# Key weights in four loads, and a new table of engine orders, in a linear-attention and gMLP kernel

## The chip, the core and the metric

The kernel runs on one core of one Trainium2 chip. Its engines are TensorE (PE, matmuls, with the loading of its weights, PEld, as a stream of its own), VectorE (DVE), ScalarE (ACT), GpSimd (POOL) and SyncE (SP, which here only issues transfers). The metric is the device time of one execution in microseconds (us). It was 242.62 us before the change, the median of three runs (242.23, 242.62 and 243.85).

## What is computed

Two residual blocks follow each other on x of 2048 rows by 512 columns. H is 32 heads of 16 columns, F is 1792 and Fh is 896.

```python
h  = x + A(layernorm(x))
h2 = h + B(layernorm(h))

def A(x):                         # linear attention
    q, k, v = split(x @ wqkv)     # 32 heads of 16 columns each
    phi = lambda t: where(t > 0, t + 1, exp(t)) + 1e-6
    kv  = einsum('bhsd,bhse->bhde', phi(k), v)
    z   = sum of phi(k) over the rows
    return ((phi(q) @ kv) / (phi(q) @ z + 1e-6)) @ wo

def B(x):                         # gMLP with a spatial mix
    z  = gelu(x @ w_in)           # 1792 columns
    z1, z2 = z[:, :896], layernorm(z[:, 896:])
    g  = w_sp @ z2 + b_sp         # w_sp is 2048 x 2048
    return (z1 * g) @ w_out
```

## The kernel before, in words

The 2048 rows are 16 tiles of 128 rows, and four groups of four tiles. Everything stays in SBUF between the load of x and the store of the result. The stages, as TensorE sees them:

- Start. Ten matmuls on a constant keep TensorE busy (L563). x arrives in loads of one, two or four tiles (the function `load_x`, issued at L495). DVE takes the statistics of each tile (L575 for the sums, L579 to put them together), the reciprocal standard deviation comes from ACT for the first four tiles (L589, L591) and from POOL for the others, in pairs (L594 adds epsilon, L596 raises to a power), and DVE normalises (L610). Tiles 0 to 3 are transposed by TensorE (L644, copied out by ACT at L651), the other twelve by transfers that SP issues (L636).
- Projections. K is x times the key weights, tile by tile (L732), and Q is computed transposed, by groups of rows (L746). ACT takes the exponential and the positive part (L709, L711) and DVE puts phi together (L712 clamps, L715 adds, L718 does the sum with a selection for pairs without a positive part from ACT). phi(k) times x is accumulated over all tiles (L764).
- The small matrices. The sum z (L776, L789), the products with the value weights (L813) and with wo (L832), the denominators (L852, their logarithm and exponential on ACT at L857 and L860), and a spreading of the reciprocals over the heads (L868, copied out by ACT at L872), by which DVE scales phi(q) (L876).
- The attention's output (L898), to which DVE adds x (L903). For the second layernorm DVE takes statistics (L575, L579), POOL makes the scale and the shift of two tiles with four instructions (L594, L596, L625, L626), ACT applies them (L617), and SP transposes the result into hT by a transfer (L636).
- z2 (L930, gelu by ACT at L935, layernorm by DVE at L939, L579 and L610 with POOL's L594 and L596), and z1 transposed (L961, gelu by ACT at L966).
- The spatial mix (L1000, its sum and product by DVE at L1007 and L1009) and the output projection (L1018, the residual at L1024, the store at L1026).

The matrix w_sp comes in by 64 transposing transfers of one 128 by 512 block each (L976), all issued by SP, 16 for each of four groups of output rows; the mix of a group waits for its 16. POOL issues the large plain loads: the value weights, wo and w_in when the last transfer that transposes x has landed, and w_out and the bias b_sp when the last transfer into hT has landed.

No planner runs when the kernel is built. The program is recorded as some 790 operations with their dependences, and a list written out in the file, ORDER, gives the order in which they are put on their engines' queues. A second list, SLOT, gives the buffer that each temporary tile takes (PSUM banks, the buffers of phi, and so on), in the order of their first use. Each engine runs its queue strictly in that order, and waits on semaphores where the data or a buffer is not there yet. The schedule does not look at costs: the numbers beside the operations (`act_c`, `dve_c`, `MM`) fill in times that decide nothing on the chip.

The loads at the start are these. SP issues x0, x2, x3, the query weights and the rest of x, and ACT issues x1 and the key weights, which are one load of 512 KB:

```python
    load_x("sp", 0, 1)
    load_x("act", 1, 2)
    load("act", "wk", wqkv[:, D:2 * D], w3[:, :, D:2 * D], D * D * 2)
    load_x("sp", 2, 3)
    load_x("sp", 3, 4)
    load("sp", "wq", wqkv[:, 0:D], w3[:, :, 0:D], D * D * 2)
```

## Time and profile before

| | |
|---|---|
| median of three runs | 242.62 us (242.23 to 243.85) |
| the profiled execution's own time | 243.94 us |
| its span, first to last instruction | 242.2 us, at a mean granted TensorE clock of 1.000 |
| VectorE busy, from 10 to 25 us | 5.00, 4.67 and 5.00 of each 5.00 us |
| matmuls of the spatial mix (L1000, two groups of rows) | 73.5 and 24.3 us busy |
| transfers that transpose into hT | 16, in the median 2.5 us from issue to landing |

The profiled execution took 243.94 us, 1.32 us more than the median of the runs without a profile and 1.74 us more than its own span. In a row of a timeline the first number is the start in us from the start of the span and the second the time to the end of the last instruction of that row; then come engine, source line, operation, what is written and read, the shapes, and the number of instructions. Brackets tell how long the engine was idle before and what ended that. A `q` behind an engine's name marks its issuing of transfers, which is not counted as busy. Matmuls overlap, so of four of 512 columns that start at 65.01 the next group can start at 65.87. A row of DMA issues ends with the median time in us from issue to landing.

Of the kernel before, what the change touches and what calls it, by code (L numbers as in the profile page):

```python
# [10 lines left out]
P = 128  # L11
# [1 line left out]


ORDER = [
# [34 lines left out]
]  # L50
SLOT = [
# [6 lines left out]
]  # L58


# [95 lines left out]
class Program:  # L156
# [14 lines left out]
    def op(self, eng, cost, fn, r=(), w=(), bias=0.0, after=(), dma=None, nbytes=0, land=2.0, lag=None,  # L171
           mode=0):
        o = Op()
        o.eng, o.fn, o.cost, o.seq = eng, fn, cost, len(self.ops)
        o.bias, o.land, lag = bias + self.bias, land, self.LAG[eng] if lag is None else lag
        o.late, o.start, o.mode = self.late, None, mode
        o.after, o.deps, o.tiles = list(after) + self.first_of.get(eng, []), {}, []
        o.marked, o.sem, o.semval, o.grp, o.bytes, o.lag = False, None, None, dma, nbytes, lag
        o.raw = set()
        for x in list(r) + list(w):  # L180
            t = getattr(x, "tile", None)
            if t is not None and t not in o.tiles:
                o.tiles.append(t)
                t.ops.append(o)
        rk = [k for x in r for k in x.keys]
        wk = [k for x in w for k in x.keys]
        for k in rk:
            p = self.writer.get(k)
            if p is not None:
                o.deps[p] = True  # L190
                o.raw.add(p)
        for k in wk:
            p = self.writer.get(k)
            if p is not None:
                o.deps[p] = True
            for q in self.readers.get(k, ()):
                if q is not o:
                    o.deps[q] = True
        for k in rk:
            self.readers.setdefault(k, []).append(o)  # L200
        for k in wk:
            self.writer[k] = o
            self.readers[k] = []
        self.ops.append(o)
        return o
# [149 lines left out]
def bass_sequential_preLN__linear_attn_block__mixer_gmlp__prompt_kernel(  # L355
# [11 lines left out]
    _, S, D = A_x.shape  # L367
# [4 lines left out]
    NT, KD, KF, NG = S // P, D // P, FH // P, S // GW  # L372
# [36 lines left out]
    wqkv = View(s_w3, 0, [KD, 3 * D], BF16)  # L409
# [84 lines left out]
    def load(eng, name, dst, src, nbytes, bias=0.0, behind=(), cost=0.5):  # L494
        o = op(eng, cost, lambda e: e.dma_start(dst.ap(), src), w=[dst], dma=(name, False), nbytes=nbytes,  # L495
               bias=bias, land=2.3)
        for p in behind:
            o.deps[p] = True
        return o

    w3 = A_wqkv.rearrange("(c p) f -> p c f", p=P)
# [3 lines left out]
    def load_x(eng, a, b, bias=BIG, **kw):  # L505
        more = {2: 40e3, 3: 60e3, 4: 70e3}.get(a, 0)
        xl[a] = load(eng, f"x{a}", x[a:b, :], x_dram[a * P:b * P, :].rearrange("(n p) d -> p n d", p=P),
                     int((b - a) * P * D * 2 + more), bias, **kw)

    load_x("sp", 0, 1)  # L510
    load_x("act", 1, 2)
    load("act", "wk", wqkv[:, D:2 * D], w3[:, :, D:2 * D], D * D * 2)
    load_x("sp", 2, 3)
    load_x("sp", 3, 4)
    load("sp", "wq", wqkv[:, 0:D], w3[:, :, 0:D], D * D * 2)
    for a in (4, 6):
# [141 lines left out]
    for grp in LN1:  # L658
# [3 lines left out]
        for n in grp:  # L662
# [6 lines left out]
            if n in CENTRED:  # L669
                m, c = st_x[n, 6:7], xc[n, :]  # L670
# [426 lines left out]
```

### The profile page before, as it was taken

Reading aid. Unit: us, or ns where it says so; the run is one execution under the profiler, and the core shown is the slowest. Engines: PE = TensorE matmul, PEld = TensorE weight load, DVE = VectorE, ACT = ScalarE, POOL = GpSimd, SP = SyncE. Lnnn points to the kernel's source line nnn. Section 1 sums busy time; section 2 is a strip of 40 time slices with the busy share of each in tenths; the row PEclk is TensorE's granted clock in tenths of the full one; section 3 lists DMA queues with packets and bytes.
Section 4 is the critical chain, followed back from the end, with each engine's and each line's share of the span. In section 5 each row is a group of like instructions: output and inputs, shape, how many; then the busy total and the mean of one; then the engine's idle time right before and its main releaser. Section 6 shows DMA issues by size and latency. Waiting matters only on the chain.

```text
span 242.2 us, 3056 instructions
## 1 busy us (share of the span) xinstructions
PE 236.3 (98%) x1191; PEld 109.8 (45%) x1191; DVE 132.7 (55%) x269; ACT 78.9 (33%) x101; POOL 36.8 (15%) x84
## 2 busy tenths in 40 slices
PE   7999999999699999999999999999999999999996
PEld 2444444544344445544444444444444444444443
DVE  4899864599967972779505333252332523322443
ACT  3794663777646798464240000000000000000000
POOL 5131314004341420436100000000000000000000
PEclk9999999999999999999999999999999999999999
DMA  6933249991543324597443444442000200000022
GB/s 219 300 79 55 43 89 244 318 132 27 64 88 69 82 46 87 103 301 112 95 108 89 91 106 104 92 110 86 0 0 0 65 24 0 0 3 0 0 87 87
DMA packets 56702, 21.83 MB, mean 90 GB/s; under 512 B 50704, under 2 KB 55824, under 8 KB 56688
## 3 DMA queue, kind: packets, MB, share of 16 engines
q1 hardware_dynamic: 54928, 16.62, 31.8%
q0 software_dynamic: 944, 4.33, 5.7%
q10 hardware_dynamic: 816, 0.70, 0.9%
q8 instruction: 9, 0.15, 0.3%
q14 instruction: 5, 0.04, 0.1%
HBM read 7.47 MB, written 2.10 MB: 40 GB/s over the span
## 4 chain that ended last, share of the span: by engine, by line
PE 91%; DMA 3%; DVE 2%; POOL 1%; ACT 1%; issue 0%; ACTq 0%
PE ps L1000 40%; PE ps L1018 10%; PE ps L961 10%; PE ps L930 9%; PE ps L764 6%; PE ps L732 6%; PE ps L746 5%; PE ps L898 4%; DMA hT<-xn 2%; DVE small L575 1%; DMA xh<-in_A_x_dram 1%; ACT xn L617 1%; DVE xh L903 1%; PE ps L832 0%; PE ps L776 0%; PE ps L813 0%
## 5 line engine op out<-in xcount | busy, mean ns | idle before, releaser
L1000 PE MATMUL ps<-wsp,pk_xn_z 128*128 128x512 bf16 x336 | 73.5, 379 | 0.0
L1007 DVE TENSOR_TENSOR e<-ps,e 128x512 bf16<-128x512 f32 x28 | 19.3, 691 | 67.4 <-PE ps L1000 67.4
L1000 PEld LDWEIGHTS ps<-wsp,pk_xn_z 128*128 128x128 bf16 x336 | 32.9, 98 | 39.7
L930 PE MATMUL ps<-win,hT 128*128 128x512 bf16 (+1 forms) x128 | 26.0, 353 | 1.9 <-DMA hT<-xn 1.9
L961 PE MATMUL ps<-hT,win 128*128 128x512 bf16 x112 | 26.1, 379 | 0.0
L1018 PE MATMUL ps<-wout,xT_pq_z 128*128 128x512 bf16 (+2 forms) x119 | 24.7, 366 | 0.0
L1000 PE MATMUL ps<-wqkv_wsp,pk_xn_z 128*128 128x512 bf16 x112 | 24.3, 379 | 0.0
L939 DVE BATCH_NORM_STATS2 small<-pk_xn_z 128x6 f32<-128x512 bf16 (+1 forms) x32 | 18.2, 607 | 9.0 <-ACT pk_xn_z L935 9.0
L575 DVE BATCH_NORM_STATS2 small<-xh 128x6 f32<-128x512 bf16 x32 | 21.0, 676 | 3.8 <-DMA xh<-in_A_x_dram 3.7
L709 ACT ACTIVATE e<-ps 128x1024 bf16<-128x1024 f32 x16 | 16.4, 1025 | 12.1 <-PE ps L732 7.6
L930 PEld LDWEIGHTS ps<-win,hT 128*128 128x128 bf16 x128 | 12.4, 98 | 14.4 <-ACT xn L617 2.0
L966 ACT ACTIVATE xT_pq_z<-ps 128x1024 bf16<-128x1024 f32 (+1 forms) x16 | 14.2, 917 | 11.4 <-PE ps L961 11.4
L1018 PEld LDWEIGHTS ps<-wout,xT_pq_z 128*128 128x128 bf16 x119 | 11.5, 98 | 13.0
L1024 DVE TENSOR_TENSOR e<-ps,xh 128x512 bf16<-128x512 f32 (+2 forms) x17 | 11.2, 660 | 11.3 <-PE ps L1018 11.3
L596 POOL TENSOR_TENSOR small<-small 128x2 f32<-128x2 f32 x22 | 17.0, 792 | 1.1
L1000 PEld LDWEIGHTS ps<-wqkv_wsp,pk_xn_z 128*128 128x128 bf16 x112 | 11.0, 98 | 13.2
L935 ACT ACTIVATE pk_xn_z<-ps 128x896 bf16<-128x896 f32 x16 | 14.3, 918 | 8.1 <-PE ps L930 8.0
L961 PEld LDWEIGHTS ps<-hT,win 128*128 128x128 bf16 x112 | 11.0, 98 | 12.7
L594 POOL TENSOR_SCALAR small<-small 128x2 f32<-128x2 f32 x22 | 6.7, 307 | 65.9 <-DVE small L579 65.8
L764 PE MATMUL ps<-pk_xn_z 128*128 128x512 bf16 x64 | 16.2, 379 | 0.0
L732 PE MATMUL ps<-wqkv_wsp,xT_pq_z 128*128 128x512 bf16 x64 | 15.9, 379 | 0.0
L746 PE MATMUL ps<-xT_pq_z,wqkv_wsp 128*128 128x512 bf16 x64 | 15.5, 380 | 0.0
(71 smaller groups left out, 181.8 us busy)
## 6 DMA issues: line engine op xcount, KB each, us to landing
out_dram<-e SPq DMA_DIRECT2D x15, 128.0 KB, 1.7
win<-in_B_w_in_dram POOLq DMA_DIRECT2D x1, 1792.0 KB, 12.3
xh<-in_A_x_dram SPq DMA_DIRECT2D x4, 256.0 KB, 6.7
wout<-in_B_w_out_dram POOLq DMA_DIRECT2D x1, 896.0 KB, 6.3
wsp<-in_B_w_sp_dram SPq DMA_TRANSPOSE x48, 2.7
wqkv_wsp<-in_A_wqkv_dram ACTq DMA_DIRECT2D x1, 512.0 KB, 4.5
wqkv_wsp<-in_A_wqkv_dram SPq DMA_DIRECT2D x1, 512.0 KB, 6.1
xh<-in_A_x_dram SPq DMA_DIRECT2D x1, 512.0 KB, 7.4
```

The source lines that it names most:

```text
L575: op("dve", dve_c(512), lambda e: e.bn_stats(s6.ap(), src.ap()), r=[src], w=[s6])
L596: return op("pool", 0.665, lambda e: e.tensor_tensor(dst.ap(), dst.ap(), h.ap(), ALU.pow), r=[dst, h], w=[dst])
L709: op("act", act_c(n), lambda e: e.activation(lo.ap(), t(flat).ap(), ACT.Exp), r=[t()], w=[lo])
L732: i = e.matmul(t(bank(ti)).ap(), lhsT=lhs.ap()[:, c, :], rhs=rhs.ap()[:, c, :], start=(c == 0), stop=(c == KD - 1))
L746: r_ = e.matmul(t(bank(i)).ap(), lhsT=lhs.ap()[:, c, :], rhs=rhs.ap()[:, c, :], start=(c == 0), stop=(c == KD - 1))
L764: r = e.matmul(txk[h](bank(i)).ap(), lhsT=xx.ap()[:, c * P:(c + 1) * P], rhs=kk.ap(), start=(n == 0), stop=(n == NT - 1))
L930: k = e.matmul(t(bank(i)).ap()[:, 0:b - a], lhsT=l.ap()[:, c, :], rhs=win[c, a:b].ap(), start=(c == 0), stop=(c == KD - 1))
L939: op("dve", dve_c(b - a), lambda e, s6=s6, src=src: e.bn_stats(s6.ap(), src.ap()), r=[src], w=[s6])
L961: k = e.matmul(t(bank(i)).ap(), lhsT=l.ap()[:, c, :], rhs=r_.ap()[:, c, :], start=(c == 0), stop=(c == KD - 1))
L1000: k = e.matmul(t(bank(0)).ap(), lhsT=l.ap()[:, s - a, :], rhs=r_.ap()[:, s - a, :], start=(s == 0), stop=(s == NT - 1))
L1007: op("dve", dve_c(512), lambda e: e.tensor_tensor(gb().ap(), t(bank(0)).ap(), bsp().ap()[:, tg * GW:(tg + 1) * GW], ALU.add), r=[t(), bsp( ...
L1018: k = e.matmul(t(bank(0)).ap()[:, 0:b - a], lhsT=l.ap()[:, fc, :], rhs=wout[fc, a:b].ap(), start=(fc == 0), stop=(fc == KF - 1))
```

## The change

The key weights come in four loads of 128 KB, one for each 128 rows of the weight matrix, all issued by ACT, and x1 moves from ACT to SP:

```diff
     load_x("sp", 0, 1)
-    load_x("act", 1, 2)
-    load("act", "wk", wqkv[:, D:2 * D], w3[:, :, D:2 * D], D * D * 2)
+    load_x("sp", 1, 2)
     load_x("sp", 2, 3)
+    for c in range(KD):
+        load("act", f"wk{c}", wqkv[c, D:2 * D], w3[:, c, D:2 * D], P * D * 2)
     load_x("sp", 3, 4)
     load("sp", "wq", wqkv[:, 0:D], w3[:, :, 0:D], D * D * 2)
 ORDER = [
-    0, 3, 4, 11, 13, 14, 1, 2, 5, 6, 7, 8, 9, 10, 16, 12, 37, 38, 27, 28, 29, 30, 31, 32, 33, 34, 21, 44, 26, 39, 40,
+    0, 1, 30, 31, 32, 33, 3, 34, 4, 5, 6, 35, 40, 41, 16, 17, 21, 2, 7, 8, 9, 29, 42, 43, 10, 11, 12, 13, 24, 14, 15,
...
```

The whole of ORDER and SLOT is replaced. No operation is added or taken away beside the three loads, so what changes is the place of each operation on its engine's queue, and the buffers. The places that matter below:

- TensorE. All four K products of tiles 0 to 3 now come before the first Q product. Between the product with wo (L832) and the first attention output (L898) stands one Q product instead of two, and between the second pair of denominators (L852) and its spreading (L868) one attention output instead of two. Behind the z2 product of tile 0 (L930, eight matmuls) came the z2 product of tile 1; now two attention outputs (L898, eight matmuls) stand between them. In both orders 352 matmuls stand ahead of tile 0's z2 product.
- DVE. The last normalisations of x come ahead of the phi of K's tiles 8 and 9, and between the statistics of attention tiles 0 and 1 stands a clamp (L712).
- POOL. The order of the large loads was value weights, wo, w_in; it is now w_in, value weights, wo. The building of the matrix for the spreading (L548, L550) moves from the start to between and behind these loads. The load of the bias b_sp comes nine operations of L594 and L596 later behind that of w_out.
- SP. Ahead of the first transfer into hT stand 13 transfers of w_sp instead of 11. The other three of the first sixteen now stand together between the fifteenth and the sixteenth transfer into hT, where they were five, spread over three places.
- ACT. The gelus and normalisations of the second half are in another order.

Lines of the changed kernel behind the loads are one higher than those given here.

72 rows, old and new, of tables (ORDER, SLOT) are left out of this document.

## The prediction

> **What bounds the kernel now.** I read the page's table of engines and its row of the granted clock first, then the waits of TensorE, then TensorE's timeline from 58 to 72 us, where its only waits of any size lie, then the chain of waits of that stretch and its transfers, and last the start and POOL's queue.
>
> ```profile
> PE 236.3 (98%) x1191; PEld 109.8 (45%) x1191; DVE 132.7 (55%) x269; ACT 78.9 (33%) x101; POOL 36.8 (15%) x84
> PEclk9999999999999999999999999999999999999999
> 58.38 0.62 PE L852 MATMUL ps<-xT_pq_z,small 128*32 128x256 bf16 x16
> 58.93 1.90 PE L898 MATMUL ps<-pk_xn_z,xT_pq_z 128*128 128x512 bf16 x8
> 60.82 0.61 PE L868 MATMUL ps<-wsp 128*128 128x128 bf16 x8
> 61.65 1.69 PE L930 MATMUL ps<-win,hT 128*128 128x512 bf16 x8 [0.23 <-DMA hT<-xn]
> 65.01 1.02 PE L930 MATMUL ps<-win,hT 128*128 128x512 bf16 x4 [1.68 <-DMA hT<-xn]
> 65.87 1.03 PE L898 MATMUL ps<-pk_xn_z,xT_pq_z 128*128 128x512 bf16 x4
> 66.74 0.81 PE L930 MATMUL ps<-win,hT 128*128 128x384 bf16 x4
> ```
>
> TensorE is 98% busy at full clock, and the change neither adds nor removes a matmul. So only TensorE's idle time can be won. After its first K product at 6.87 it waits twice to speak of: 0.23 us ahead of z2 of tile 0 and 1.68 ahead of z2 of tile 1. Tile 0's eight matmuls cost 0.86 (65.01 to 65.87, four of 512 columns) and, for its four of 384 columns, three quarters of 0.87 (65.87 to 66.74), 0.65, so 1.51 together. They could have been over at 61.65 + 1.51 = 63.16, and tile 1 starts at 65.01: 1.85 us lost. With the 0.23, some 2.1 us, 0.9% of the time, is all that the change can win.
>
> ```profile
> 52.44 1.24 DVE xh L903
> ...
> 55.30 0.86 POOL small L594
> ...
> 57.70 0.63 POOL small L626
> 58.35 1.52 ACT xn L617 x2
> ...
> 60.45 4.43 DMA hT<-xn
> ```
> ```profile
> hT<-xn SPq DMA_TRANSPOSE x1, 2.4
> ```
> ```profile
> q8 instruction: 1, 0.02, 2.9%
> ```
>
> This chain of waits releases tile 1. Its last step is a transfer that took 4.43 us. The one before it, for tile 0, issued in 59.00 to 60.42 and shown second, took 2.4. The third fence is the table of DMA queues from 62 to 64: one packet of 20 KB of instructions or less was fetched just then, behind which part of the late transfer stood. At 2.4 us tile 1 would have landed at 62.85 and nothing would have been lost. So 1.85 us hangs on one accident of a profiled execution, which took 243.94 us, 1.32 above the median. I do not know whether it is in the unprofiled runs (242.23, 242.62, 243.85 differ by as much), and count two thirds of it there: 1.24 us in the median.
>
> **The change, part by part.** *Start.*
>
> ```profile
> 3.38 0.69 DVE L575 BATCH_NORM_STATS2 small<-xh 128x6 f32<-128x512 bf16 x1 [3.38 <-DMA xh<-in_A_x_dram]
> 4.39 0.29 ACT L589 ACTIVATE small<-small 128x1 f32<-128x1 f32 x1 [1.39 <-DVE small L579]
> 4.21 0.66 DVE L575 BATCH_NORM_STATS2 small<-xh 128x6 f32<-128x512 bf16 x1
> 5.38 0.66 DVE L575 BATCH_NORM_STATS2 small<-xh 128x6 f32<-128x512 bf16 x1
> 6.48 0.66 DVE L575 BATCH_NORM_STATS2 small<-xh 128x6 f32<-128x512 bf16 x1
> 6.87 1.03 PE L732 MATMUL ps<-wqkv_wsp,xT_pq_z 128*128 128x512 bf16 x4
> 1.23 0.46 ACTq L495 DMA_DIRECT2D wqkv_wsp<-in_A_wqkv_dram  x1
> 1.72 1.28 ACT L554 ACT_TABLE_LOAD   x1 [1.72 <-PEq L1082]
> ```
> ```profile
> xh<-in_A_x_dram SPq DMA_DIRECT2D x2, 128.0 KB, 3.5
> wqkv_wsp<-in_A_wqkv_dram ACTq DMA_DIRECT2D x1, 512.0 KB, 4.5
> ```
>
> The first K product follows x0's statistics at 3.38 through normalising, transposing and copying, and x0 is still the first load. ACT now issues four loads, the first in place of x1, so the second ends at 1.69, the last 2 x 0.46 later at 2.61, and the table load at 3.9, ahead of 4.39. The key weights landed at 1.23 + 4.5 = 5.73; with x1 and x2 six pieces of 128 KB came in behind x0's 3.38, 0.39 us each. Now x0, key piece, x1, key piece and so on alternate. At 0.39 each x1 lands at 4.2, x2 at 4.9, x3 at 5.7 and the last key piece at 6.1, against uses at 4.21, 5.38, 6.48 and 6.87. I cost the start at 0; the cover is these margins, and where it is gone, one issue (0.46) goes straight onto the path: 0 to +0.45. SP's queue issues x1 as well, so query weights and later x leave up to 0.45 later. The query weights have gained time, as all four K products now stand ahead of the first Q: 0.
>
> *POOL's loads* are one queue, with a new order.
>
> ```profile
> 36.29 0.98 POOL L495 DMA_DIRECT2D wqkv_wsp<-in_A_wqkv_dram  x1 [4.87 <-DMA xT_pq_z<-pk_xn_z]
> 37.28 0.76 POOL L495 DMA_DIRECT2D wqkv_wsp<-in_A_wo_dram  x1
> 38.03 0.75 POOL L495 DMA_DIRECT2D win<-in_B_w_in_dram  x1
> ```
> ```profile
> win<-in_B_w_in_dram POOLq DMA_DIRECT2D x1, 1792.0 KB, 12.3
> wqkv_wsp<-in_A_wqkv_dram POOLq DMA_DIRECT2D x1, 512.0 KB, 5.0
> wqkv_wsp<-in_A_wo_dram POOLq DMA_DIRECT2D x1, 512.0 KB, 6.2
> ```
> ```profile
> 45.47 1.06 PE L813 MATMUL ps<-wsp,wqkv_wsp 128*128 128x128 bf16 x16
> 47.77 1.06 PE L832 MATMUL ps<-wqkv_wsp,wsp 128*32 128x512 bf16 x16
> ```
> ```profile
> 27.21 0.43 DVE L712 TENSOR_SCALAR e<-e 128x1024 bf16<-128x1024 bf16 x1 [0.54 <-ACT e L709]
> 27.67 1.23 DVE L718 SCALAR_TENSOR_TENSOR pk_xn_z<-ps,e 128x1024 bf16<-128x1024 f32 x1
> ```
>
> The three landed 4.95, 7.2 and 14.04 us behind the first issue (38.03 + 12.3 = 50.33). In proportion to bytes win alone takes 1792/2816 x 14.04 = 8.9 and each small one 2.5. The small ones now come last: from 36.29, value weights near 47.8 and wo at 50.33. Their products stood at 45.47 and 47.77. By matmuls ahead they move to about 46.3 and 48.4, so TensorE would lose up to 1.9 us (all of it by wo). But the last normalisations of x no longer stand behind a clamp and a sum (0.43 + 1.23 = 1.66), so the last transposes, and the loads, can start up to 1.7 earlier. Then 0.2 is left. The cost lies between 0 and 1.9; I take 0.4, nearer to the early start, since the queue order that makes it is certain and only POOL's part of that chain can spoil it. Building the spreading matrix behind these loads, and b_sp nine operations later, fall in time that POOL idles (15% busy): 0.
>
> *The chain to z2 of tile 0.*
>
> ```profile
> 55.70 0.42 DVE L712 TENSOR_SCALAR e<-e 128x1024 bf16<-128x1024 bf16 x1
> ```
> ```profile
> 77.33 0.22 POOL L594 TENSOR_SCALAR small<-small 128x2 f32<-128x2 f32 x1 [6.88 <-DVE small L579]
> ...
> 78.73 0.20 POOL L626 TENSOR_TENSOR small<-small 128x2 f32<-128x2 f32 x1
> ```
> ```profile
> 34.82 19.90 SPq L976 DMA_TRANSPOSE wsp<-in_B_w_sp_dram  x11
> ```
>
> One clamp (0.42) now stands among the statistics of the pair, and the step at 55.30 begins near 55.75. Matmuls ahead of z2 of tile 0 stay 352, so its wait grows by this: +0.45 (0 if the chain beats TensorE by other means, 0.9 if two such operations slip in). POOL's four instructions took 3.03 us there (55.30 to 58.33) and 1.6 at 77.33 to 78.93, alone. I keep 3.03, since DVE again adds and clamps beside them. The Trainium skill, "SBUF — State Buffer", section Who interferes with whom, says that a DVE instruction with two SBUF inputs, or in a two-port mode, shares ports with POOL's reads. By that rule POOL stays slow and the sum stands; by the calm row tile 0 would land 1.4 earlier and 0.45 would go. SP has 13 w_sp transfers ahead of tile 0's instead of 11, at 1.81 each (19.90/11): begun at 34.8 they are out by 58.4, before ACT's first half at 58.35 + 0.76 = 59.1, and cost 0.
>
> Behind z2 of tile 0 now stand eight attention matmuls: 2 x 0.87 = 1.73 us of cover. Even a transfer of 4.4 us hardly shows: -1.85 in the profile, -1.24 in the median.
>
> *The rest.* One attention product instead of two between denominators and spreading, and gelus in another order: margins of tenths, no priced wait. From nothing to a few; I take one wait like the smallest seen, +0.23.
>
> **Sum.** 0 + 0.4 + 0.45 + 0.23 = 1.08. The profiled execution: 243.94 - 1.85 + 1.08 = 243.17. Against the median: 242.62 - 1.24 + 1.08 = **242.5**.
>
> A rule speaks against the split. The Trainium skill, "DMA: Bandwidth & Descriptors", section Bandwidth, asks for transfers of 1 MiB or more and gives 0.95 us for 64 KB alone; my estimate from that page is at least 0.95 us for each piece, 3.8 in a row. By that the last lands near 3.38 + 3.8 = 7.2 us, 0.3 late, and the sum is 242.8. The rows lean the other way: pieces in flight together came in 0.39 apart.
>
> **The rivals.**
> 1. *The small weights starve behind win* (slower than before). For it: one queue, win's 12.3 us. Against it: the earlier normalisations. wo comes 1.9 late instead of 0.4: 242.5 + 1.5 = 244.0. It decides from 0.56 us late on, where the sum passes 242.62; beyond 3 us late the time passes +1%. If win's 12.3 us must be over first, then 2.25 each (7.2 less 4.95), wo lands at 36.29 + 12.3 + 4.5 = 53.1, 4.7 late: 246.8.
> 2. *The transfer's accident does not recur anyway*, or falls where nothing covers it: no 1.24. For it: a fetch of instructions depends on the engines' progress. 242.5 + 1.24 = 243.7.
> 3. *All new orders are hidden* and both waits go: 242.62 - 1.85 - 0.23 = 240.5. For it: the 2.1 us are in this trace; against it, the clamp and win.
> 4. *Small pieces are slow at the start*: one issue, 0.45, on the path: 242.9. For it: x1's margin is nothing. Against it: the last key piece's is 0.8.
>
> **How the numbers follow.** Chances: forecast 0.44, rival 1 0.22, rival 2 0.17, rival 3 0.10, rival 4 0.07. The likeliest is 242.5, its own range 242.0 to 243.4 (the chain from 0 to 0.9, the rest at its value; the start's 0.45 is rival 4). One per cent, about what a measurement of this kernel can tell from no change, is 240.2 to 245.05. Faster by more needs more than rival 3: 0.06. Slower by more needs half of rival 1 (0.11) or it together with rival 2 or 4 (0.06): 0.17. Within: 0.77. The range 240.5 to 245.0 leaves out some 0.2.
>
> **What would show it.** Right: K's first product within 0.3 of 6.87; z2 of tile 0 near 62.1 with under 1 us of idle, and none over 0.3 ahead of tile 1; L813 and L832 (now L814, L833) wait at most 0.5 for their loads. Wrong: wo lands after 49, TensorE idle at L833; a first K product past 7.3 that waits for a key piece; a wait of TensorE above 1 us at L931, or anywhere behind 67 us, where it had none.

## The result, and the profile after

The changed kernel takes 244.28 us (median of 20 runs, 243.38 to 246.23), the kernel before 242.63 (20 runs, 241.99 to 244.70): a ratio of 1.0067, interval 1.0042 to 1.0092. It is slower by 0.7%, and the rise is clear of the noise; 242.5 was forecast, next to no change, in a range of 240.5 to 245.0. The profiled execution took 245.65 us, 1.71 more than the profiled one before.

The page of the changed kernel, first part, and the granted clock in 40 slices:

```profile
PE 237.6 (97%) x1191; PEld 110.6 (45%) x1191; DVE 133.0 (55%) x269; ACT 78.9 (32%) x101; POOL 36.9 (15%) x84
PEclk9799999999999999999999999999999999999999
```

The matmuls are the same, and yet TensorE is busy 1.3 us longer: in the second slice its clock is down. The start shows why. From the timelines of VectorE and TensorE of the changed kernel, the statistics of x2, the transposition of tile 1, and the first K product:

```profile
6.43 0.69 DVE L576 BATCH_NORM_STATS2 small<-xh 128x6 f32<-128x512 bf16 x1 [1.03 <-DMA xh<-in_A_x_dram]
...
7.49 0.46 PE L645 MATMUL ps<-small,pk_xn_z 128*128 128x128 bf16 x4 [1.44 <-DVE pk_xn_z L611]
7.95 1.91 PE L733 MATMUL ps<-wqkv_wsp,xT_pq_z 128*128 128x512 bf16 x4
```

The statistics of x2 began at 5.38 before, without a wait; now x2 lands at 6.40 instead of 3.87, and they begin at 6.43. VectorE's queue has them ahead of the normalisation of tile 1, so tile 1 is late. TensorE's queue has the transposition of tile 1 ahead of the first K product, which starts at 7.95 instead of 6.87. Its four matmuls take 1.91 us instead of 1.03: TensorE sat idle for 1.44 us and lost its rate. The view by windows, from 5 to 10 us (busy time of each engine, then the granted clock, the DMA share and GB/s), of the kernel before and then of the changed one:

```profile
5.00:10.00 5.00, 4.18 (x32) 2.21 (x32) 4.00 (x11) 3.78 (x11) 0.00 (x0) 1.00 1.08 354
```
```profile
5.00:10.00 5.00, 3.11 (x18) 1.65 (x19) 2.99 (x9) 2.49 (x8) 0.00 (x0) 0.77 1.00 341
```

The clock is 0.77 there. From 7.70 it is at half for 3.41 us, which costs 1.7 us. Over the whole span it is 0.993 in this execution; so it is in five of the 20 runs (0.992 or 0.993), those at 245.65 to 246.23. The other fifteen, at 0.999 or 1.000, took 243.38 to 244.89.

TensorE around z2 of tiles 0 and 1 in the changed kernel:

```profile
62.53 1.04 PE L899 MATMUL ps<-pk_xn_z,xT_pq_z 128*128 128x512 bf16 x4
64.11 0.62 PE L869 MATMUL ps<-wsp 128*128 128x128 bf16 x8 [0.55 <-ACT wsp L861]
65.25 1.67 PE L931 MATMUL ps<-win,hT 128*128 128x512 bf16 x8 [0.51 <-issue]
66.76 1.89 PE L899 MATMUL ps<-pk_xn_z,xT_pq_z 128*128 128x512 bf16 x8
68.48 1.68 PE L931 MATMUL ps<-win,hT 128*128 128x512 bf16 x8
```

The wait of 1.68 us ahead of tile 1's z2 is gone: it starts at 68.48, straight behind the attention matmuls. In its place stand two waits ahead of tile 0's, 0.55 and 0.51. The chain of waits that leads there, in the changed kernel:

```profile
57.13 0.33 DVE e L713
...
58.43 0.57 POOL small L595
...
59.08 1.02 POOL small L597
...
60.17 0.80 POOL small L626
...
61.04 0.67 POOL small L627
...
61.73 1.52 ACT xn L618 x2
63.25 0.37 ACT wsp L858
63.62 0.02 issue
63.64 0.42 ACT wsp L861
64.07 0.04 issue
64.11 0.62 PE ps L869 x8
```

The clamp L713 stands in it, as forecast; but POOL's four instructions take 3.28 us (58.43 to 61.71), not 3.03, and from the residual (L904 at 55.18) to ScalarE's normalisation it is 6.55 us, where it was 58.35 - 52.44 = 5.91.

### The profile page after: what moved, and what is told of

Its sections match the earlier page's. It is cut to its first block, busy times and chain, and to the rows that moved or that the text cites. A ratio compares the mean times of both kernels' runs of the same rounds, so it can differ in the third digit from the quotient of the medians.

```text
span 243.9 us, 3053 instructions
## 1 busy us (share of the span) xinstructions
PE 237.6 (97%) x1191; PEld 110.6 (45%) x1191; DVE 133.0 (55%) x269; ACT 78.9 (32%) x101; POOL 36.9 (15%) x84
## 4 chain that ended last, share of the span: by engine, by line
PE 92%; DMA 2%; DVE 2%; POOL 1%; ACT 1%; issue 1%; SPq 0%
PE ps L1001 40%; PE ps L931 10%; PE ps L1019 10%; PE ps L962 10%; PE ps L733 6%; PE ps L765 6%; PE ps L747 5%; PE ps L899 4%; DMA xh<-in_A_x_dram 2%; DVE small L576 1%; ACT xn L618 1%; DVE xh L904 1%; PE ps L869 0%; PE ps L645 0%; POOL small L597 0%
## 5 line engine op out<-in xcount | busy, mean ns | idle before, releaser
L733 PE MATMUL ps<-wqkv_wsp,xT_pq_z 128*128 128x512 bf16 x64 | 17.0, 404 | 0.0
```

The source lines that it names most:

```text
L733: i = e.matmul(t(bank(ti)).ap(), lhsT=lhs.ap()[:, c, :], rhs=rhs.ap()[:, c, :], start=(c == 0), stop=(c == KD - 1))
```

## The experiments

Each comparison is with the kernel before, run beside it on the same chip. Its own times come in two heaps: of 160 runs in all, 45 took 243.4 us or more and most others 242.0 to 242.7, so its median moves between 242.2 and 242.6.

**1. The start alone, and the order alone.** The loads are set back in the new order, and the new loads are put into the old order; the rest of each order is kept.

```diff
-    load_x("sp", 1, 2)
+    load_x("act", 1, 2)
+    load("act", "wk", wqkv[:, D:2 * D], w3[:, :, D:2 * D], D * D * 2)
     load_x("sp", 2, 3)
-    for c in range(KD):
-        load("act", f"wk{c}", wqkv[c, D:2 * D], w3[:, c, D:2 * D], P * D * 2)
```

> The changed kernel with the start of the kernel before: x1 and one key load of 512 KB by ScalarE, everything else of the new order kept. Theory START (the lost time is made by the loads at the start: x2 lands at 6.40 instead of 3.87, the first K product stands at 7.95 instead of 6.87): x2 lands by 4.5, the first K product is back within 0.2 of 6.87, no matmul of K at half rate, and the time falls by 1.1 to 1.6 us from 244.3 to about 242.9; TensorE still waits about 0.9 us ahead of z2 of tile 0. Rival ORDER (the new order itself is what is slower, the late start is swallowed later): the time stays at 244 or above.

> The kernel before with the changed start alone: x1 by SP, four key loads by ScalarE, the old order of the rest. START: x2 lands near 6.4, the first K product starts 0.9 to 1.2 us later than 6.87, and the time rises by 1.0 to 1.6 us to 243.7 to 244.2. ORDER: no change from 242.6, as the start has 0.4 us of slack at each load.

Measured: the start undone 243.3 us (12 runs), ratio 1.0031, 1.0006 to 1.0057; the start alone 242.91, ratio 1.0028, 0.9997 to 1.0059; the kernel before 242.19. Neither theory is enough: by the medians the start costs 0.7 us and the order 1.1, and together they make the change. (The interval of the start alone just takes in no change; that its first K product is late its trace shows.) In the kernel with the start undone:

```profile
6.99 1.03 PE L733 MATMUL ps<-wqkv_wsp,xT_pq_z 128*128 128x512 bf16 x4
...
62.83 1.67 PE L931 MATMUL ps<-win,hT 128*128 128x512 bf16 x8 [0.63 <-issue]
```

The first K product is back (6.99), at full rate, and z2 of tile 0 starts at 62.83, 1.18 later than the 61.65 of the kernel before. With the start alone the first K product stood at 7.67, 0.80 late, and in 4 of 12 runs the mean clock was 0.993.

**2. Why x2 is late.** Two changes of the loads in the changed kernel: the key weights in one load again, with x1 still by SP; and four pieces, with x1 by ScalarE.

```diff
-    for c in range(KD):
-        load("act", f"wk{c}", wqkv[c, D:2 * D], w3[:, c, D:2 * D], P * D * 2)
+    load("act", "wk", wqkv[:, D:2 * D], w3[:, :, D:2 * D], D * D * 2)
```
```diff
-    load_x("sp", 1, 2)
+    load_x("act", 1, 2)
```

> The changed kernel with the key weights in one load of 512 KB again, but x1 still by SP ahead of x2, so that x2 is the third load of its queue. Theory THIRD (a queue's third load lands about 2.4 us behind its second, however many loads there are: x3 in the kernel before landed at 6.12 as SP's third, x2 in the changed one at 6.40 as SP's third): x2 still lands at 6.0 to 6.5, the first K product near 7.9, the time stays at 244.0 to 244.4. Rival PIECES (the four small key loads slow everything that is in flight): x2 lands near 4.5, the first K product near 6.9, the time is about 242.9.

> The changed kernel with x1 moved back to ScalarE ahead of the four key pieces, so that x2 is SP's second load and three of the key pieces are ScalarE's third to fifth. THIRD: x2 lands near 4, and the key pieces from the second on come late, at 6.2 to 7.5, so that the first K product waits for the last piece until 7.0 to 7.6, and the time is 0.5 us or more under 244.3. PIECES: x2 stays late, at 5.5 or above, as the number and size of the loads is the same, and the time stays near 244.3.

Measured: one key load 245.86 us (6 runs), ratio 1.0122, 1.0081 to 1.0163; x1 by ScalarE 246.82, ratio 1.0175, 1.0127 to 1.0222. Both times lie above all that either theory had forecast, and above that of the change itself (though the intervals of the first and of the change touch); in 4 and in 5 of the 6 runs the clock was lowered. x1 in the first of them (VectorE's timeline), then the loads and the first K product in the second (median us from issue to landing):

```profile
5.61 0.69 DVE L576 BATCH_NORM_STATS2 small<-xh 128x6 f32<-128x512 bf16 x1 [1.43 <-DMA xh<-in_A_x_dram]
```
```profile
wqkv_wsp<-in_A_wqkv_dram ACTq DMA_DIRECT2D x4, 128.0 KB, 5.6
...
xh<-in_A_x_dram SPq DMA_DIRECT2D x3, 128.0 KB, 2.9
```
```profile
8.80 1.02 PE L733 MATMUL ps<-wqkv_wsp,xT_pq_z 128*128 128x512 bf16 x4 [1.59 <-ACT small L592]
```

With one key load x2 landed at 5.96, though there are no pieces. But x1, SP's second load, was late too, behind the 512 KB issued ahead of it (at 0.81; from 3 to 4 us ScalarE's queue alone moved anything): bytes issued ahead count as well, which the theory of the third load did not say. With x1 by ScalarE x2 landed at 4.16, as forecast by that theory, and the key pieces from the second on at 7.28, 7.88 and 8.72, later than forecast.

This second kernel and the one with the start undone issue the same loads in the same places; only the key weights come in four pieces or in one. So the two show what the split does by itself: x3 lands at 7.08 instead of 6.03, and the time is 246.82 us instead of 243.3. In between the transfers run slower. From 4 to 5 us, in the kernel before, the changed one and the one with x1 by ScalarE (the last number is GB/s):

```profile
4.00:5.00 1.00, 1.00 (x3) 0.15 (x1) 0.88 (x4) 0.50 (x2) 0.34 (x1) 1.00 1.03 348
```
```profile
4.00:5.00 1.00, 0.84 (x3) 0.14 (x1) 0.95 (x4) 0.50 (x2) 0.00 (x0) 1.00 0.74 167
```
```profile
4.00:5.00 1.00, 1.00 (x3) 0.15 (x1) 0.89 (x3) 0.96 (x3) 0.00 (x0) 1.00 0.37 111
```

All five kernels with four key pieces show this slow microsecond (111 to 193 GB/s), and none of the other fifteen (348 to 386). PIECES is therefore not refuted; it is only too coarse, as x2 escapes when it is issued at 1.24. Why the transfers slow down is not shown. By their medians the two steps of the new start, x1 by SP and the split, each cost more alone (ratios of 1.0122 and 1.0175) than together (1.0067).

To part bytes from places, x0 of the kernel before is loaded in two halves:

```diff
-    load_x("sp", 0, 1)
+    for h in range(2):
+        load("sp", f"x0{h}", x[0, h * 256:h * 256 + 256], x_dram[0:P, h * 256:h * 256 + 256], P * D)
```

> The kernel before with the load of x0 issued by SP as two halves of 64 KB, nothing else changed, so that x2 becomes SP's third load and x3 its fourth; the bytes ahead of x2 stay the same. THIRD (a queue's third load lands at about 6.0 or later, some 2 us behind its second): x2 lands at 5.7 to 6.5 instead of 3.87, the first K product starts 0.8 to 1.1 us later than 6.87, the time rises by 0.7 or more. Rival BYTES (what counts is how many bytes were issued ahead): x2 lands at 3.9 to 4.5, the first K product stays within 0.2 of 6.87, the time stays at 242.2.

Measured: 244.47 us (10 runs), ratio 1.0072, 1.0037 to 1.0107. VectorE's statistics of x0 and x2:

```profile
4.21 0.69 DVE L577 BATCH_NORM_STATS2 small<-xh 128x6 f32<-128x512 bf16 x1 [4.21 <-DMA xh<-in_A_x_dram]
...
6.24 0.69 DVE L577 BATCH_NORM_STATS2 small<-xh 128x6 f32<-128x512 bf16 x1
```

x2 landed at 6.21 instead of 3.87, as the third load of its queue. (x0's second half came 0.8 us late as well, at 4.19, so the time holds more than x2's share.) But bytes and places are not parted by this: as the third load x2 is issued at 1.71 instead of 1.24, and so no longer beside the 512 KB, issued at 1.23, but behind them. From 3.5 to 4.5 us 287 of the 289 packets moved were ScalarE's. In the kernel before x3 waited in the same way: in that stretch only ScalarE's queue moved anything, and x3 landed 0.37 us behind the key weights (6.12 and 5.75). In all 20 traces of this case no queue's third load landed before 5.88, while a second load of 128 KB landed at 3.87 to 4.77, unless the 512 KB stood ahead of it. Each of those third loads was issued at 1.70 or later, behind the 512 KB or into the slow microsecond; that its place in the queue makes it late is not shown.

**3. What x2's lateness costs.** In the changed kernel, once the places of tile 1 are taken out from behind x2 in three queues (normalisation, copy and K product of tile 1 ahead of the work on tile 2), and once TensorE is kept busy over the wait:

```diff
-    for gate, n, cost, count in ((tr_op[0], 512, MM, 1), (tr_op[1], 256, MM / 2, 1)):
+    for gate, n, cost, count in ((tr_op[0], 512, MM, 7), (tr_op[1], 256, MM / 2, 1)):
```

The first of the two changes only ORDER: `44, 48, 54, 49, 50, 51` becomes `44, 48, 49, 50, 51, 54`, `46, 130, 56, 57, 53` becomes `46, 53, 130, 56, 57`, and 59 moves behind 131.

> The changed kernel, its loads as they are, with four places in the order changed: VectorE normalises tile 1 ahead of the statistics of x2, ScalarE copies tile 1's transpose out ahead of the logarithm for x2, and TensorE does tile 1's K product ahead of the transposition of tile 2. START, with the loss made by VectorE standing at the statistics of x2 and TensorE's work queued behind it: the first two K products run from about 6.9 to 8.7 although x2 still lands near 6.0 to 6.4, the loss at the start falls from 1.1 us to 0.5 or less, the time falls by 0.6 to 1.2 us to about 243.3. Rival: the key pieces themselves are what is late (the last landed at 7.33 in the changed kernel): the first K product cannot start before 7.3 and the time falls by 0.5 at most.

> The changed kernel with six more matmuls on a constant between the transposes of tiles 0 and 1, so that TensorE is not idle for 1.44 us there. If idleness is what halves the rate of the K products (0.43 us for each instead of 0.22 in the profiled execution): all K products at 0.22, a mean granted clock of 1.000 in all runs, the first K product still at about 7.9, and no run of 245.6 or more (5 of 20 before); the median falls by a few tenths, to about 244.0. Rival (the rate is lost by chance, whatever TensorE does): the share of such runs stays.

Measured: tile 1 ahead 244.47 us (12 runs), ratio 1.0086, 1.0057 to 1.0115; kept busy 244.25 (243.78 to 244.76), ratio 1.0050, 1.0027 to 1.0074; before 242.51. TensorE with tile 1 ahead, then the window from 5 to 10 us of the kernel kept busy:

```profile
7.35 1.89 PE L734 MATMUL ps<-wqkv_wsp,xT_pq_z 128*128 128x512 bf16 x8 [0.28 <-issue]
...
10.15 1.90 PE L734 MATMUL ps<-wqkv_wsp,xT_pq_z 128*128 128x512 bf16 x8
```
```profile
5.00:10.00 5.00, 4.76 (x29) 2.53 (x29) 3.36 (x10) 3.17 (x9) 0.00 (x0) 1.00 1.04 351
```

With tile 1 ahead the rival was right: the first product waits for the last key piece (7.26) and starts at 7.35. And the third product still waits for x2 and x3, until 10.15: moving the queues wins nothing, because both x2 and x3 are late. Kept busy, TensorE runs at a clock of 1.00 in that window, and all 12 runs have a mean clock of 1.000, none above 244.76, against five of 20 above 245.6 (and 25 of 66 runs with a lowered clock in the six kernels with a late start). So the half rate comes of the idle stretch; the Trainium skill, "TensorE: Matmul & The Clock Gate", section What's actually happening, tells of such a gate that follows TensorE's recent activity, and these runs agree.

**4. The path to z2 of tile 0.** In the new order on the old start, the clamp is taken from between the statistics (ORDER, in the numbers of the changed kernel):

```diff
-    293, 296, 260, 297, 294, 295,
+    293, 296, 294, 297, 295, 260,
```

> The new order with the start of the kernel before (as in the first experiment, 243.3), and the clamp L713 taken from between the statistics of attention tiles 0 and 1 to behind them, as in the old order. Theory CHAIN (the rest of what the new order loses is the path to z2 of tile 0, of which the clamp is 0.4): z2 of tile 0 starts 0.3 to 0.45 us earlier than 62.83 against the first K product, and the time falls as much, to about 242.9. Rival (TensorE waits there for the spreading or another thing, the clamp is covered): no change.

Measured: 243.36 us (12 runs), ratio 1.0006, 0.9974 to 1.0038. Against the 243.3 of the first experiment nothing is won. ScalarE and TensorE:

```profile
58.17 1.52 ACT L618 ACTIVATE xn<-xh,small 128x512 bf16<-128x512 bf16 x2 [0.92 <-POOL small L627]
```
```profile
62.80 1.67 PE L931 MATMUL ps<-win,hT 128*128 128x512 bf16 x8 [1.10 <-DVE small L580]
```

ScalarE's normalisation came 1.03 us earlier (59.20 with the clamp between), more than the clamp's 0.42. But the transfer of tile 0, issued at 59.01, took 3.7 us and landed at 62.70, 0.10 ahead of z2 (the row names another releaser): a 16 KB packet of instructions was fetched at 60.19 and held one DMA engine for 0.92 us. That is the accident that I had seen on tile 1. In every trace one such fetch lies between TensorE's 314th and 365th recorded matmul (warming ones that were added not counted), about where the first transfers into hT run. I tried to move it by cutting the ten warming matmuls at the start into more, shorter ones:

```diff
-    WARM = 10
+    WARM = 28
...
-        warm = [keep_busy(512, MM, warm)]
+        warm = [keep_busy(176, MM, warm)]
```

First in the old order (28 of 176 columns, and 16 of 310), then in the new one (18 of 280), with the clamp behind and between:

> The kernel before with its ten warming matmuls of 512 columns at the start cut into 28 of 176, the same work in more instructions. In each trace so far one packet of 16 KB of instructions is fetched when TensorE stands at its 336th to 356th matmul, 60 to 63 us into the span, and holds one DMA engine for about 1 us. Theory FETCH (the late transfers into hT, and the runs of the kernel before at 243.4 to 244.0, come of this fetch, whose place hangs on the count of TensorE's instructions): 18 more matmuls ahead move it to about 58.5 to 59.5, clear of both transfers; z2 of tile 1 no longer waits, and all but a run or so lie at 242.0 to 242.5, none at 243.4 or above. Rival (the transfers are late by chance): about a third of the runs stay at 243.4 or above.

> The kernel before with its warming matmuls cut into 16 of 310 columns, so that the fetch of instructions moves six matmuls earlier, to about 60.5 to 61.3, on the transfer into hT of tile 0, which landed at 61.60. FETCH: tile 0's transfer takes 3.4 us or more instead of 2.4, z2 of tile 0 waits 1 us or more instead of 0.23, and the median rises to 243.2 or above. Rival (chance): the times are those of the kernel before, with a median of 242.2 to 242.6.

> The new order with the start of the kernel before and the clamp behind the statistics (243.36; its transfer of tile 0 took 3.7 us with the fetch at 60.19 upon it), and eight more, shorter warming matmuls. FETCH: the fetch moves to 58.0 to 59.0, ahead of tile 0's transfer, which takes 2.4 to 2.6 us; z2 of tile 0 starts near 61.5 instead of 62.80 and the time falls by 1.0 to 1.3 us to 242.0 to 242.3, without runs above 243.4. That would be the best version. Rival (the path to z2 of tile 0 is late for another reason): it stays at 243.2 to 243.5.

> The same eight shorter warming matmuls, with the clamp still between the statistics. In the first experiment tile 0's transfer took only 2.6 us, so moving the fetch wins nothing there: CHAIN and FETCH together say 243.2 to 243.4 and z2 of tile 0 near 62.7 to 62.9, so that the difference to the kernel with the clamp behind is the clamp's own cost, 1.0 us by the start of ScalarE's normalisation (59.20 against 58.17). Rival (the clamp costs its 0.42 us and no more): 242.5 to 242.7.

Measured, against 242.2: 242.74 us (242.54 to 243.40; ratio 1.0014, 0.9999 to 1.0030), 242.5 (1.0018, 0.9991 to 1.0046), 243.87 (1.0087, 1.0054 to 1.0119) and 243.38 (1.0052, 1.0030 to 1.0073). My forecast of where the fetch goes was wrong in two of four: with 16 it went to 64.02, later instead of earlier, so nothing could be doubled there; with 18 in the new order it stayed at 60.25, on tile 0's transfer, and z2 of tile 0 started at 63.47. With 28 in the old order it went to 57.40 and no run of 12 lay above 243.40, where 5 of 24 beside it did; but the first fetch had moved as well, to 16.03, onto a transfer of x, and TensorE waited 0.4 us there. How the count sets the place stays open. Whether the place sets the time was tried with three more counts (28 of 176, 13 of 394, 23 of 222) in the new order on the old start with the clamp behind, and with 23 in the old order:

> The new order with the old start and the clamp behind the statistics, with the warming matmuls cut into 28 of 176 columns. FETCH: in the old order this count brought the third fetch to 57.40; if it lies before 59.1 here, tile 0's transfer takes 2.4 to 2.6 us, z2 of tile 0 starts at 61.4 to 61.8 instead of 62.80, and the time is 242.0 to 242.5 unless the first fetch now stands on a transfer of x (0.5 us more, as in the old order); if the fetch lies at 59.5 to 61.4, the time stays at 243.2 or above. Rival (z2 of tile 0 is held by another thing): 62.8 wherever the fetch lies.

> The same kernel with 13 warming matmuls of 394 columns. FETCH: where the third fetch lies is not forecast, its effect is: outside 59.5 to 61.4 us z2 of tile 0 starts at 61.4 to 61.8 and the time is 242.0 to 242.5; within it the transfer takes 3.2 us or more and the time is 243.2 or above. Rival: no such link.

> The same kernel with 23 warming matmuls of 222 columns; expected as for 13 of them: 242.0 to 242.5 where the third fetch lies outside 59.5 to 61.4 us, 243.2 or above within it.

> The kernel before with 23 warming matmuls of 222 columns. FETCH: if the third fetch leaves the stretch from 60.3 to 62.9 us, in which the transfers of tiles 0 and 1 run, no run lies at 243.4 or above, and the median is 242.0 to 242.3, or 242.7 where the first fetch stands on a transfer of x; if it stays in it, a third or more of the runs are late by 1.4 to 1.9 us.

Measured, against 242.5: 242.45 us (242.03 to 243.16; ratio 0.9978, 0.9951 to 1.0005), 243.88 (1.0024, 0.9998 to 1.0050), 243.59 (1.0035, 1.0011 to 1.0060) and 242.43 (1.0004, 0.9975 to 1.0032). Queues and issues of the kernel with 28 from 58.9 to 60.2, and TensorE; then, of the kernel with 13, the queues from 60.9 to 62.4, the transfer of tile 0, issued at 59.10, and TensorE:

```profile
q8 instruction: 1, 0.02, 4.5%
issues: line engine op xcount, KB each, median us to landing
hT<-xn SPq DMA_TRANSPOSE x1, 2.4
```
```profile
62.18 1.68 PE L932 MATMUL ps<-win,hT 128*128 128x512 bf16 x8
```
```profile
q1 hardware_dynamic: 523, 0.13, 109.8%
q8 instruction: 1, 0.02, 4.6%
```
```profile
hT<-xn SPq DMA_TRANSPOSE x1, 4.3
```
```profile
63.49 1.67 PE L931 MATMUL ps<-win,hT 128*128 128x512 bf16 x8 [1.71 <-DVE xT_pq_z L877]
```

With 28 the fetch (59.07) is the only packet of its stretch, tile 0 takes 2.4 us, and TensorE does not wait. With 13 and 23 (fetch at 61.11 and 60.09) it stands among the transfer's packets, the transfer takes 4.3 and 4.2 us, and TensorE waits 1.7 and 1.6. The same kernel, then, moves by 1.1 to 1.4 us with the place of one fetch. With 23 in the old order the fetch was at 59.46, ahead of tile 0's packets, in the profiled execution; 5 of 12 runs were late all the same, and what happened in those no trace shows.

The last two kernels, both with 28 warming matmuls: two accumulations (145, 147 in the changed kernel's numbers) moved ahead of the K product of tile 6 (158), which had waited 0.50 us for its transfer; and the clamp back between the statistics.

```diff
-    ... 148, 158, 145, 159, 239, 155, 147, ...
+    ... 148, 145, 147, 158, 159, 239, 155, ...
```

> The new order with the old start, the clamp behind the statistics and 28 warming matmuls (242.45, from 242.03 to 243.16), and two accumulations of phi(k) times x (of tiles 2 and 3, 0.43 us each) moved ahead of the K product of tile 6, which waited 0.50 us for its transfer. If that wait was a cost of its own: no wait there, and 241.9 to 242.1 in most runs, none above 243.2, against 242.2 to 242.5 for the kernel before. If what is won there is given back at z2 of tile 0: no change, 242.4.

> The new order with the old start and 28 warming matmuls, the clamp left between the statistics of attention tiles 0 and 1; it differs from the kernel of 242.45 by the clamp's place alone. CHAIN: ScalarE's normalisation starts 1.0 us later (59.8 instead of 58.83), z2 of tile 0 starts 0.9 to 1.0 us later than 62.18, and the time is 243.3 to 243.6. Rival (the clamp costs its own 0.42 us): 242.8 to 242.9.

Measured, against 242.23: 242.17 us (242.02 to 244.61, 11 of 12 runs up to 242.60), ratio 0.9992, 0.9965 to 1.0018; and 243.52 (243.22 to 244.03), ratio 1.0045, 1.0027 to 1.0063. ScalarE and TensorE with the clamp between:

```profile
59.91 1.52 ACT L619 ACTIVATE xn<-xh,small 128x512 bf16<-128x512 bf16 x2 [1.92 <-POOL small L628]
```
```profile
63.26 1.67 PE L932 MATMUL ps<-win,hT 128*128 128x512 bf16 x8 [0.34 <-issue]
```

The clamp's place alone is 59.91 - 58.83 = 1.08 us at ScalarE, 63.26 - 62.18 = 1.08 at TensorE, and 243.52 - 242.45 = 1.07 in the medians: one to one. (0.09 us of it were there already at the residual ahead of the clamp, 53.36 against 53.27.) In the first of the two TensorE waits nowhere behind its first K product, and yet the time is that of the earlier heap of the kernel before. No wait is left there that an order could win; no version beat the kernel before by more than the noise.

## Why the prediction was wrong, point by point

- *The start at 0* failed, and it is the first of the two steps that made the sign wrong; the second is the cover at -1.24. "At 0.39 each x1 lands at 4.2, x2 at 4.9, x3 at 5.7 and the last key piece at 6.1": they landed at 4.00, 6.40, 7.11 and 7.33. The first four loads came faster than that (0.29 each from 3.37 to 4.24), and then nothing landed for over 2 us. The 0.39 was read with one key load of 512 KB in flight, and holds there: x3 landed 0.37 behind the key weights (6.12 and 5.75). With the split it does not hold: from 4 to 5 us 167 GB/s moved instead of 348, and what stood behind the first two loads of each queue came late. Nor had I looked at each landing. The 3.5 us that I quoted for two x loads is the median of 2.6 and 4.4. The second load took 2.6 and the third took 4.4; a window from 2 to 3 us shows the third by itself, in the kernel before:

```profile
xh<-in_A_x_dram SPq DMA_DIRECT2D x1, 128.0 KB, 4.4
```

  and in the changed kernel the three loads of each queue that are issued from 1.6 to 2.3 us:

```profile
xh<-in_A_x_dram SPq DMA_DIRECT2D x3, 128.0 KB, 4.7
wqkv_wsp<-in_A_wqkv_dram ACTq DMA_DIRECT2D x3, 128.0 KB, 4.9
```

  x3 could bear to land so late, as it was used last; x2, moved into its place, could not. Rival 4 named the place and the pieces, but as one issue, of 0.45 us. Bounded by "one issue (0.46)", the start cost 1.08 us at the first K product, and in a quarter of the runs about 1.7 more through the clock, for which no term stood in the sum. The Trainium skill's rule for large loads ("DMA: Bandwidth & Descriptors", section Bandwidth), which I weighed, did point the right way: by it the last piece lands near 7.2, and it landed at 7.33. But the pieces did not come evenly, as that estimate has it, and in the changed kernel it was x2 that held TensorE, not the last piece.
- *POOL's loads at 0.4* were 0. The issues and the two products in the changed kernel:

```profile
win<-in_B_w_in_dram POOLq DMA_DIRECT2D x1, 1792.0 KB, 8.1
wqkv_wsp<-in_A_wqkv_dram POOLq DMA_DIRECT2D x1, 512.0 KB, 9.0
wqkv_wsp<-in_A_wo_dram POOLq DMA_DIRECT2D x1, 512.0 KB, 9.2
```
```profile
48.97 1.06 PE L814 MATMUL ps<-wsp,wqkv_wsp 128*128 128x128 bf16 x16
...
51.04 1.06 PE L833 MATMUL ps<-wqkv_wsp,wsp 128*32 128x512 bf16 x16
```

  The weights landed at 46.66 and 48.34, over 2 us ahead; with the start undone too (43.99 and 45.71 against 46.44 and 48.51). All three took 11.6 us from the first issue instead of 14.04. The issue came earlier, and by more than the 1.7 worked out (34.23 with the start undone, 2.1 earlier). Rival 1 is refuted.
- *The chain to z2 of tile 0 at +0.45* was the right mechanism at half its size: 0.87 us in this profile, and about 1.0 for the clamp's place by itself. The clamp's own part was 0.39 in both comparisons (from the residual to POOL's first instruction 3.25 us instead of 2.86), about as put; the step that failed is "I keep 3.03": with the clamp between, POOL's four instructions took 3.27 us, with it behind 2.66 (the two kernels with 28 warming matmuls). In the changed kernel they took 3.28, 0.25 more than before, and the remaining 0.2 lie behind ScalarE's normalisation, where the transfer of tile 0 took 2.58 us instead of 2.42. VectorE adds, multiplies and clamps beside them in both, but shifted by one operation. This fits the ports that VectorE and POOL share by the Trainium skill ("SBUF — State Buffer", section Who interferes with whom); which pairs meet was not tried.
- *The cover behind z2 of tile 0 at -1.24* was right in its mechanism, wrong in its size. No trace of the new order waits ahead of tile 1. But at most 45 of 160 runs of the kernel before were late by it, so in a median it is worth at most the 0.4 between 242.63 and 242.2, not two thirds of 1.85. Nor is the fetch itself an accident: it comes in the same stretch of matmuls in all 20 traces. What decides in which runs it hurts is not shown. Rival 2 named it ("falls where nothing covers it"), and in four kernels of the new order it fell late on the transfer of tile 0 (3.7 to 4.4 us).
- *Small waits later at +0.23*: none. Behind 67 us TensorE waits for nothing in the changed kernel. The two waits at 64.11 and 65.25 belong to the chain.
- *The sum*, put right: 242.2 for the earlier heap of the kernel before, + 1.08 for the start, + 0.87 for the chain in this profile (z2 of tile 0 is 10.10 us behind the end of the second attention output, where it was 9.23) = 244.15, against 244.00 in the median of the fifteen runs at full clock and 244.28 in that of all 20.

## What to carry to other kernels

A rate that was read with one large load in flight need not hold once that load is split: look at each landing by itself, and at what the transfers move in the stretch that decides. Loads that are issued later than before, behind a large one or in the place of another, have to be priced by the landings of those that stood there. A short operation slipped into a chain that ends last can cost more than its own length, because the operations of another engine run beside it; price the whole chain from the last time it ran in that company. And when TensorE's work is the same and it is 98% busy, an order can win only its waits, while each new wait, at the start above all, can cost twice, by the idle time and by the rate that is lost with it.

## What the runs showed of the hardware that I had not expected

- One packet of 16 KB of instructions, fetched for 0.9 to 1.6 us on one DMA engine, made a transposing transfer of 2.4 us last 3.7 to 4.4 where it began 1.2 to 2.1 us behind the issue of the transfer (six traces, on tile 0 or 1); where it began at most 0.4 us behind the issue of tile 0's, that took 2.6 to 3.1 (eight traces, the changed kernel's among them). The Trainium skill, "Runtime: NRT & Kernel Launch", section Instruction fetch mechanics, states pages of that size and calls their cost mostly hidden; here no wait of TensorE of over 0.2 us stands at such a fetch in the kernels before and after, but for those on the transfers beside it. The number of warming matmuls changed which transfer it met, in a way that I could not forecast.
- With the same loads in the same places, the key weights in four pieces instead of one took what the transfers moved between 4 and 5 us from 385 GB/s to 111 (the kernels with the start undone and with x1 by ScalarE).
- Idle stretches of 0.62 and 1.44 us at the start, with short work between, were followed by half rate (0.43 us for a matmul of 512 columns instead of 0.22) for 3.41 us in the profiled execution; by their clock, four more of the 20 runs lost as much.
